# Parking 384 more floats of kept V in PSUM and in the pT tiles while the first MLP streams its weights

## Chip, cores and metric

One NeuronCore of a Trainium2 chip. The metric is the time of one execution in device microseconds (us). A *float* below is one 4-byte number in each of the 128 partitions, so a stretch of n floats is n x 512 bytes.

## What is computed

Two rounds of the same attention block and the same gated MLP on a batch of 4 tokens of width 640. All inputs are float32. The caches and the weights are the same in both rounds.

```python
def attention(x):                       # 32 heads of 128, the last W=1024 rows of the cache
    q = (x @ wq).reshape(B, 1, 32, 128).transpose(0, 2, 1, 3)
    k, v = k_cache[:, :, -W:], v_cache[:, :, -W:]
    p = softmax(einsum("bhqd,bhkd->bhqk", q, k) * 128 ** -0.5)
    o = einsum("bhqk,bhkd->bhqd", p, v)
    return o.transpose(0, 2, 1, 3).reshape(B, 1, 4096) @ wo
def mlp(x):                             # F = 1728
    gate, up = x @ W_gate, x @ W_up
    return (gate * (gate > 0) * up) @ W_down
for _ in range(2):
    x = x + attention(layernorm(x))
    x = x + mlp(layernorm(x))
```

## The kernel before

**What is streamed.** Nearly all the work is reading weights and caches from HBM. The host lays them out in three rows of floats per partition: `heads` (255,744 floats: W_q, K, V and W_o of 27 heads, in the order of their use), `kept` (47,360 floats: the same of the last five heads) and `mlp` (25,920 floats). Layer 0 and layer 1 each read `heads` and `mlp`. `kept` is read once, in layer 0, and stays on the chip until layer 1 has used it. The first `HELD` = 4288 floats of `heads`, a piece of W_q, go to a tile of their own, `first_q`, and stay there for layer 1 too.

**The ring.** Everything else goes through one tile, `store`, of `STORE` = 50,624 floats. Before the kernel is written out, a list `plan` is made of (layer, row, from, to, place in `store`): the pieces, one DMA each, in the order in which they are loaded. `load()` (lines 212 to 221) issues the next piece on SyncE's (SP's) queue as soon as no float of its place in `store` is still in use (`live`). `done()` marks what a matmul has just read as free and calls `load()`. So the order of the DMAs is fixed. On the chip SP takes them one by one, and an issue that waits for TensorE (PE) to finish with a place keeps all later ones waiting.

**The kept part and the first MLP.** In layer 0's MLP `kept` fills 47,360 of the 50,624 floats (`FRONT` is its end). The MLP's 25,920 floats have to pass through what is left, and three stretches of `kept` are moved out of the way for that time: `AHEAD` (768 floats, moved to `probs`), `BACK` (1600 floats of V, moved to the PSUM tile `ps` and to idle columns of `po` and `yy`) and `AWAY` (1408 floats of V just below `BACK`, moved to `parked`, which is 640 columns of the PSUM tile `pp`, and to 384 columns in each of the two `banks`). ScalarE (ACT) makes all these copies. `AWAY` is copied out at the end of layer 0's attention (lines 463 and 529 to 532, then `free(*AWAY)`) and back into `store` late in the MLP (lines 609 to 613); `BACK` comes back in layer 1. The pieces of the MLP are listed by hand in `gu` (used twice for the gate and up weights), `gu_end` and `wd` (W_down); together 7040 floats of places are in rotation. After them come the first pieces of layer 1's `heads`, written out the same way.

**pT.** `pT` is a pair of SBUF tiles of 140 columns that hold the transposed probabilities; VectorE (DVE) writes four columns of each sixteen (line 450), and the columns between must be zero. They are idle from the end of layer 0's attention until layer 1's first values.

**Engines.** PE multiplies; DVE and ACT do softmax, norms and copies; GpSimd (POOL) does nothing after the start.

Of the kernel before, what the change touches and what calls it, by code (L numbers as in the profile page):

```python
# [13 lines left out]
B, D, H, DH, W, F = 4, 640, 32, 128, 1024, 1728  # L14
P = 128
# [44 lines left out]

HELD = 4288
STORE = 50624
FRONT = KEPT * 2 * (D + KV)
# [3 lines left out]
BACK = FRONT - 2 * KV - 1600, FRONT - 2 * KV  # L67
AWAY = BACK[0] - 1408, BACK[0]
HOME = 12992
# [38 lines left out]
def decode_kernel(ctx: ExitStack, tc: tile.TileContext, x, source, sel, out):  # L108
# [60 lines left out]

    f, z, a, q, k = FRONT, STORE - D, AHEAD[0], AWAY[0], BACK[0]  # L170
    assert STORE - FRONT == 2 * 1280 + 64 + D
    gu = [(z, D), (f, 1280), (f + 1280, 1344), (a, 768), (k, 960), (k + 960, 640), (q, 1408)]
    gu_end = [(f, 1280), (f + 1280, 1280), (f + 2560, D)]
    wd = [(a, D), (k, 960), (k + 960, D), (q, 1280), *gu_end, (a, D), (k, D), (k + D, D)]
    lo = 0
# [5 lines left out]

    lo = HELD
    for to, n in (f, 1280), (f + 1280, 1280), (f + 2560, D + 64), (a, 768), (k, 1600):
        put(1, "heads", to, lo, lo + n)
        lo += n
# [112 lines left out]
    pp = ps_p.tile([P, 2, 512], F32, name="pp")  # L298
    parked = pp.rearrange("p j n -> p (j n)")[:, 256:896]
    po = ps_o.tile([P, 512], F32, name="po")  # L300
# [115 lines left out]
    def scores(layer, g):  # L416
        n = len(HEADS[g])
        to = sc[g] = pp if layer and g == order[1][0] else ps
        for i, h in enumerate(HEADS[g]):
            for j in range(2):  # L420
                for b in range(B):
                    lo = (j * B + b) * 512
                    at = SIDE - 1 + SIDE * (B * i + b) - i
                    product(to[32 * b:32 * b + SIDE, j, :], qT[:, at:at + SIDE], *part(layer, "k", h, lo, 512),
                            start=i == 0, stop=i == n - 1, tile_position=(0, 32 * b))
                    part_done(layer, "k", h, lo, 512)
                    if to is pp and k0 + i * KV + lo < HOME + BACK[1] - BACK[0] <= k0 + i * KV + lo + 512:
                        nc.scalar.copy(store[:, HOME:HOME + 1024], ps.rearrange("p j n -> p (j n)"))
                        nc.scalar.copy(store[:, HOME + 1024:HOME + 1280], po[:, 256:])
                        nc.scalar.copy(store[:, HOME + 1280:HOME + 1600], yy[:, QUARTER:3 * QUARTER])  # L430
        nm[g] = small.tile([P, 1], F32, name="nm", bufs=1)
# [10 lines left out]
    def values(layer, g, last=False):  # L442
# [18 lines left out]
        if last and layer == 0:  # L461
            nc.scalar.copy(po[:, 256:], store[:, BACK[0] + 1024:BACK[0] + 1280])
            nc.scalar.copy(parked, away[:, :640])
            free(*BACK)
# [26 lines left out]
    def attention(layer):  # L491
# [12 lines left out]
        for before, g, after, then in zip([None] + gs, gs, gs[1:] + [None], gs[2:] + [None] * 2):  # L504
            totals(g)
            turned()
            if layer == 0 and after is None:
                nc.scalar.copy(probs[:, QUARTER:QUARTER + 768], store[:, AHEAD[0]:AHEAD[1]])
                nc.scalar.copy(ps.rearrange("p j n -> p (j n)"), store[:, BACK[0]:BACK[0] + 1024])
                nc.scalar.copy(yy[:, QUARTER:3 * QUARTER], store[:, BACK[1] - 320:BACK[1]])  # L510
                free(*AHEAD)
# [17 lines left out]
        if layer == 0:  # L529
            for i in range(2):  # L530
                nc.scalar.copy(banks[i][:, P:], away[:, 640 + 384 * i:1024 + 384 * i])
            free(*AWAY)
            project(layer, gs[-2])
# [3 lines left out]
    def forward(layer):  # L537
# [71 lines left out]
        if layer == 0:  # L609
            nc.scalar.copy(away[:, :640], parked)  # L610
            for i in range(2):
                nc.scalar.copy(away[:, 640 + 384 * i:1024 + 384 * i], banks[i][:, P:])
            live[AWAY[0]:AWAY[1]] = [True] * 1408
        down(1)
# [64 lines left out]
```

## Time and profile before

| | |
|---|---|
| time, median of 3 runs | 731.91 us (731.81 to 732.6) |
| the profiled execution's own time | 731.96 us |
| its span (first to last instruction) | 730.2 us |
| read from HBM | 310.57 MB |
| PE busy | 443.9 us (61%) |
| DVE, ACT busy | 76.1 us, 54.5 us |

The profile lists the busy time of each engine, the DMA queues with their bytes and packets, and the chain of work that ended last. The trace beside it answers for any stretch: the busy time of each engine, the mean busy share of the 16 DMA engines and what they moved, who waited for whom, and for a DMA the time from its issue on SP to its landing. The profiled execution took 731.96 us with a span of 730.2 us, so 1.76 us lie outside the span.

### The profile page before, as it was taken

Reading aid. Unit: us, or ns where it says so; the run is one execution under the profiler, and the core shown is the slowest. Engines: PE = TensorE matmul, PEld = TensorE weight load, DVE = VectorE, ACT = ScalarE, POOL = GpSimd, SP = SyncE. Lnnn points to the kernel's source line nnn. Section 1 sums busy time; section 2 is a strip of 40 time slices with the busy share of each in tenths; the row PEclk is TensorE's granted clock in tenths of the full one; section 3 lists DMA queues with packets and bytes.
Section 4 is the critical chain, followed back from the end, with each engine's and each line's share of the span. In section 5 each row is a group of like instructions: output and inputs, shape, how many; then the busy total and the mean of one; then the engine's idle time right before and its main releaser. Section 6 shows DMA issues by size and latency. Waiting matters only on the chain.

```text
span 730.2 us, 8291 instructions
## 1 busy us (share of the span) xinstructions
PE 443.9 (61%) x3776; PEld 147.1 (20%) x3776; DVE 76.1 (10%) x277; ACT 54.5 (7%) x101; POOL 0.2 (0%) x4
## 2 busy tenths in 40 slices
PE   0845665654646565519878896365656556555576
PEld 0211111111111111103344241021111112111233
DVE  1110001010010101002111211001010010101011
ACT  0200000000000000000412210000000000000110
POOL 0000000000000000000000000000000000000000
PEclk9976788877777776759999999677777778878899
DMA  9999999999999999999999999999999999999996
GB/s 409 446 393 446 442 439 437 419 436 439 432 428 429 417 456 424 443 413 429 420 409 396 432 429 446 442 436 424 432 431 443 436 430 423 446 432 432 416 427 286
DMA packets 13290, 311.17 MB, mean 426 GB/s; under 512 B 1476, under 2 KB 1732, under 8 KB 6984
## 3 DMA queue, kind: packets, MB, share of 16 engines
q1 hardware_dynamic: 13104, 310.56, 99.0%
q8 instruction: 29, 0.48, 0.2%
q10 hardware_dynamic: 152, 0.09, 0.1%
q14 instruction: 5, 0.04, 0.0%
HBM read 310.57 MB, written 0.08 MB: 425 GB/s over the span
## 4 chain that ended last, share of the span: by engine, by line
DMA 77%; PE 20%; another core or an unknown queue 1%; issue 1%; DVE 0%; ACT 0%; SPq 0%; DVEq 0%; ACTq 0%
DMA store<-in_heads 60%; PE ps L252 9%; DMA store<-in_kept 8%; DMA store<-in_mlp 8%; PE po L252 5%; PE m L252 2%; PE y L252 1%; PE pp L252 1%; PE pp L440 1%; PE m L411 1%; PE m L477 0%; PE m L468 0%; PE m L349 0%; PE y L379 0%
## 5 line engine op out<-in xcount | busy, mean ns | idle before, releaser
L252 PE MATMUL po<-store,pT 128*16 128x512 f32 (+1 forms) x1026 | 156.0, 716 | 122.4 <-DMA store<-in_heads 117.0
L252 PE MATMUL ps<-store,qT 128*4 128x512 f32 (+3 forms) x996 | 151.0, 687 | 109.5 <-DMA store<-in_heads 87.9
L252 PEld LDWEIGHTS po<-store,pT 128*16 128x16 f32 x1026 | 34.4, 110 | 230.8 <-issue 110.7
L252 PEld LDWEIGHTS ps<-store,qT 128*4 128x4 f32 x996 | 30.0, 93 | 213.2 <-DMA store<-in_heads 98.9
L432 DVE TENSOR_REDUCE nm<-ps 128x1 f32<-128x1024 f32 x17 | 20.8, 1225 | 241.0 <-PE ps L252 241.0
L436 ACT ACTIVATE probs<-ps,nm 128x1024 f32<-128x1024 f32 x17 | 18.9, 1114 | 327.2 <-DVE nm L432 327.2
L252 PE MATMUL m<-store,xT 128*32 128x512 f32 (+4 forms) x150 | 29.0, 580 | 10.5 <-DMA store<-in_heads 10.3
L450 DVE COPY pT<-pp 128x16 f32<-128x16 f32 x128 | 17.2, 169 | 137.5 <-PE po L252 137.5
L460 ACT COPY gates<-po 128x512 f32<-128x512 f32 x18 | 10.5, 586 | 268.3 <-PE po L252 268.3
L252 PE MATMUL y<-store,oT 128*4 128x160 f32 x514 | 22.8, 309 | 9.6 <-DMA store<-in_heads 8.4
L440 PE MATMUL pp<-sel_sb,probs 128*128 128x128 f32 x144 | 20.4, 289 | 0.0
L470 DVE RECIPROCAL r<-m 128x16 f32<-128x16 f32 x18 | 4.6, 258 | 132.2 <-PE m L468 132.2
L440 PEld LDWEIGHTS pp<-sel_sb,probs 128*128 128x128 f32 x144 | 17.9, 151 | 0.0
L252 PE MATMUL pp<-store,xT 128*32 128x256 f32 (+3 forms) x172 | 14.3, 417 | 4.7 <-DMA store<-in_mlp 4.7
L252 PEld LDWEIGHTS y<-store,oT 128*4 128x4 f32 x514 | 12.7, 88 | 17.3 <-DMA store<-in_heads 8.8
L404 DVE TENSOR_SCALAR gates<-m,rstd 128x512 f32<-128x512 f32 (+2 forms) x18 | 12.4, 690 | 24.3 <-PE m L252 24.0
L477 PE MATMUL m<-sel_sb,gates 128*128 128x128 f32 x72 | 11.8, 291 | 1.1 <-ACT gates L460 1.1
L411 PE MATMUL m<-sel_sb,gates 128*128 128x128 f32 x64 | 12.4, 318 | 0.0
L327 PE MATMUL y<-probs,sel_sb 4*4 4x160 f32 x8 | 0.7, 445 | 18.0 <-DMA sel_sb<-in_sel 18.0
L411 PEld LDWEIGHTS m<-sel_sb,gates 128*128 128x128 f32 x64 | 7.7, 157 | 19.2 <-issue 18.8
L252 PE MATMUL y<-store,gates 128*4 128x160 f32 x192 | 9.6, 299 | 2.4 <-DMA store<-in_mlp 2.2
L252 PEld LDWEIGHTS m<-store,xT 128*32 128x32 f32 x150 | 6.2, 116 | 22.0 <-DMA store<-in_heads 12.5
(79 smaller groups left out, 143.5 us busy)
## 6 DMA issues: line engine op xcount, KB each, us to landing
store<-in_heads SPq DMA_DIRECT2D x17, 7936.0 KB, 45.8
store<-in_heads SPq DMA_DIRECT2D x2, 8160.0 KB, 44.5
store<-in_heads SPq DMA_DIRECT2D x2, 8128.0 KB, 35.9
store<-in_heads SPq DMA_DIRECT2D x2, 7968.0 KB, 36.3
store<-in_heads SPq DMA_DIRECT2D x1, 8096.0 KB, 26.3
store<-in_heads SPq DMA_DIRECT2D x1, 7424.0 KB, 44.1
store<-in_heads SPq DMA_DIRECT2D x1, 7360.0 KB, 35.4
store<-in_heads SPq DMA_DIRECT2D x1, 7168.0 KB, 35.1
```

The source lines that it names most:

```text
L252: nc.tensor.matmul(out[:, a:z], by, t[rows, p:p + z - a], start=start and not a, stop=stop and z == n, **how)
L327: nc.tensor.matmul(y[32 * g:32 * g + B], ident[:B, :B], probs[:B, g * QUARTER:(g + 1) * QUARTER], start=True, stop=True, tile_position=(0, ...
L404: nc.vector.tensor_scalar(gates[:, :len(HEADS[g]) * P], qp.pop(g), rstd, SCALE, op0=ALU.mult, op1=ALU.mult)
L411: nc.tensor.transpose(qt[:, i], gates[:, i * P:(i + 1) * P], ident)
L432: nc.vector.tensor_reduce(nm[g], to.rearrange("p j n -> p (j n)"), axis=AX.X, op=ALU.max, negate=True)
L436: nc.scalar.activation(probs, sc.pop(g).rearrange("p j n -> p (j n)"), AF.Exp, bias=nm.pop(g), accum_out=sums[g])
L440: nc.tensor.transpose(pp[:, c // 4, c % 4 * P:c % 4 * P + P], probs[:, c * P:(c + 1) * P], ident)
L450: nc.vector.tensor_copy(to[:, 4 * j:4 * j + 4], pp[:, j].rearrange("p (c x) -> p c x", c=4)[:, :, i:P:32])
L460: nc.scalar.copy(gates, po)
L470: nc.vector.reciprocal(r[g], so.rearrange("p (b i) -> p i b", b=B)[:, :SIDE])
L477: nc.tensor.transpose(ot[:, 127 * b:127 * b + P], gates[:, b * P:(b + 1) * P], ident)
```

## The change

`first_q` grows by 384 floats (`HELD` 4288 to 4672), and `store` shrinks by the same (`STORE` 50,624 to 50,240). To keep 7040 floats of places in rotation during the first MLP, `AWAY` grows by 384 floats (1408 to 1792). They go to 128 more columns of `pp` (`parked` is now 768 columns) and to the first 128 columns of each `pT`; after the copy back those columns are set to zero on POOL, since layer 1 wants them zero. The hand-written pieces follow the new places. Which floats of `BACK` and `AWAY` go to which PSUM tile is also reordered.

```diff
-HELD = 4288
-STORE = 50624
+HELD = 4672
+STORE = 50240
...
-AWAY = BACK[0] - 1408, BACK[0]
+AWAY = BACK[0] - 1792, BACK[0]
...
-    assert STORE - FRONT == 2 * 1280 + 64 + D
-    gu = [(z, D), (f, 1280), (f + 1280, 1344), (a, 768), (k, 960), (k + 960, 640), (q, 1408)]
-    gu_end = [(f, 1280), (f + 1280, 1280), (f + 2560, D)]
-    wd = [(a, D), (k, 960), (k + 960, D), (q, 1280), *gu_end, (a, D), (k, D), (k + D, D)]
+    assert STORE - FRONT == 2 * 1280 + 320
+    gu = [(z, D), (f, 1152), (f + 1152, 1088), (a, 768), (k + 448, 1152), (k - D, 1088), (q, 1152)]
+    gu_end = [(f, 1408), (f + 1408, 1472), (k - 512, 320)]
+    wd = [(a, D), (k, 960), (k + 960, D), (q, 1280), (f, 1280), (f + 1280, 1280), (f + 2560, 320), (k, 320), (a, D),
+          (k + 320, D), (k + 960, D)]
...
-    for to, n in (f, 1280), (f + 1280, 1280), (f + 2560, D + 64), (a, 768), (k, 1600):
+    for to, n in (f, 1280), (f + 1280, 1280), (f + 2560, 320), (a, 768), (k, 1600):
         put(1, "heads", to, lo, lo + n)
...
-    parked = pp.rearrange("p j n -> p (j n)")[:, 256:896]
+    parked = pp.rearrange("p j n -> p (j n)")[:, 256:]
...
-            nc.scalar.copy(parked, away[:, :640])
+            nc.scalar.copy(parked, away[:, 1024:])
             free(*BACK)
...
             for i in range(2):
-                nc.scalar.copy(banks[i][:, P:], away[:, 640 + 384 * i:1024 + 384 * i])
+                nc.scalar.copy(banks[i][:, P:], away[:, 256 + 384 * i:640 + 384 * i])
+            for i in range(2):
+                nc.scalar.copy(pT[i][:, :P], away[:, P * i:P * i + P])
             free(*AWAY)
...
-            nc.scalar.copy(away[:, :640], parked)
+            nc.scalar.copy(away[:, 1024:], parked)
             for i in range(2):
-                nc.scalar.copy(away[:, 640 + 384 * i:1024 + 384 * i], banks[i][:, P:])
-            live[AWAY[0]:AWAY[1]] = [True] * 1408
+                nc.scalar.copy(away[:, 256 + 384 * i:640 + 384 * i], banks[i][:, P:])
+                nc.scalar.copy(away[:, P * i:P * i + P], pT[i][:, :P])
+                nc.gpsimd.memset(pT[i][:, :P], 0.0)
+            live[AWAY[0]:AWAY[1]] = [True] * (AWAY[1] - AWAY[0])
```

On ACT, between the last values of layer 0's attention and the norm ahead of the MLP, these copies stand before (`m` is the pair of banks; line 357 is the norm's first copy):

```order
L462 COPY po<-store 128x256 [waits Activation_49]
L463 COPY pp<-store 128x640 [waits DVE_49,PE_49]
L531 COPY m_109<-store 128x384
L531 COPY m_110<-store 128x384 [waits DVE_49]
L357 COPY probs<-y 128x160 [waits DVE_49]
```

and these now:

```order
L463 COPY po<-store 128x256 [waits Activation_49]
L464 COPY pp<-store 128x768 [waits DVE_49,PE_49]
L532 COPY m_109<-store 128x384
L532 COPY m_110<-store 128x384 [waits DVE_49]
L534 COPY pT_98<-store 128x128
L534 COPY pT_99<-store 128x128
L358 COPY probs<-y 128x160 [waits DVE_49]
```

The copy into `pp` is 128 columns wider, and two copies of 128 columns stand ahead of the release of `AWAY` and of the norm's copy. On the way back ACT gains the same two copies, and POOL two memsets.

On SP, where the second round of the gate and up weights ends and W_down begins, the queue holds before:

```order
L221 DMA store<-in_mlp 128x1280 [waits DMAHW5_49,PE_49]
L221 DMA store<-in_mlp 128x1280 [waits DMAHW6_49,DMAHW4_49,PE_49]
L221 DMA store<-in_mlp 128x640
L221 DMA store<-in_mlp 128x640 [waits DMAHW7_49,PE_49]
L221 DMA store<-in_mlp 128x960 [waits DMAHW0_49,PE_49]
L221 DMA store<-in_mlp 128x640 [waits DMAHW1_49,PE_49]
```

and now:

```order
L222 DMA store<-in_mlp 128x1408 [waits DMAHW6_49,DMAHW5_49,PE_49]
L222 DMA store<-in_mlp 128x1472 [waits DMAHW4_49,PE_49]
L222 DMA store<-in_mlp 128x320 [waits DMAHW1_49,PE_49]
L222 DMA store<-in_mlp 128x640 [waits DMAHW7_49]
L222 DMA store<-in_mlp 128x960 [waits DMAHW0_49,PE_49]
L222 DMA store<-in_mlp 128x640
```

The third piece of this stretch went to the end of `store`, which was free by then; now it is 320 floats that go into `AWAY` (`k - 512`) and wait until PE has read that place, with the pieces for `AHEAD` and `BACK` behind it. In all SP issues 92 DMAs where it issued 91: 28 for the first MLP where there were 27, and otherwise as many as before.

## Rows read from the trace of the kernel before

**Rows 1.** The page: busy time, DMA busy share in 40 slices, DMA totals and queue.

```profile
PE 443.9 (61%) x3776; PEld 147.1 (20%) x3776; DVE 76.1 (10%) x277; ACT 54.5 (7%) x101; POOL 0.2 (0%) x4
DMA  9999999999999999999999999999999999999996
q1 hardware_dynamic: 13104, 310.56, 99.0%
HBM read 310.57 MB, written 0.08 MB: 425 GB/s over the span
```

**Rows 2.** Windows by stage: us, busy us by engine, PEclk, DMA share, GB/s.

```profile
0.00:2.00 2.00, 0.00 (x0) 0.00 (x0) 0.96 (x5) 0.00 (x0) 0.20 (x4) 1.00 0.37 74
2.00:350.00 348.00, 193.77 (x1449) 57.70 (x1450) 33.13 (x117) 19.99 (x33) 0.00 (x0) 0.78 1.00 432
350.00:400.00 50.00, 41.45 (x509) 20.05 (x507) 6.66 (x26) 12.43 (x27) 0.00 (x0) 1.00 1.01 407
400.00:700.00 300.00, 187.15 (x1480) 58.10 (x1483) 31.08 (x115) 19.14 (x33) 0.00 (x0) 0.81 1.00 433
```

**Rows 3.** The page: the chain that ended last, by engine.

```profile
DMA 77%; PE 20%; another core or an unknown queue 1%; issue 1%; DVE 0%; ACT 0%; SPq 0%; DVEq 0%; ACTq 0%
```

**Rows 4.** SP's own queue in 100 to 300 us: packets, MB, share of 16 engines.

```profile
q1 hardware_dynamic: 1673, 86.33, 99.8%
```

**Rows 5.** The same in 350 to 400 us, where the first MLP streams.

```profile
q1 hardware_dynamic: 5132, 20.28, 100.4%
```

**Rows 6.** ACT's timeline around the first MLP: start us, us, what, idle before.

```profile
354.37 0.83 ACT L508 COPY probs<-store 128x768 f32<-128x768 f32 x1 [0.49 <-PE pp L440]
...
362.18 0.69 ACT L463 COPY pp<-store 128x640 f32<-128x640 f32 x1
362.80 0.89 ACT L531 COPY m<-store 128x384 f32<-128x384 f32 x2
365.23 0.29 ACT L357 COPY probs<-y 128x160 f32<-128x160 f32 x1 [1.54 <-DVE ones L356]
...
396.48 0.29 ACT L357 COPY probs<-y 128x160 f32<-128x160 f32 x1 [5.20 <-DVE ones L356]
```

**Rows 7.** The chain in order of time, from the first MLP on: start us, us, what.

```profile
362.26 8.50 DMA store<-in_mlp
...
415.53 0.09 DVE pT L450
```

**Rows 8.** Groups by line and shape: memsets of DVE and POOL, mean ns of one.

```profile
L295 DVE MEMSET pT<- 128x140 f32 x2 | 0.3, 175 | 0.0
...
L669 POOL MEMSET const-float32-0.0<- 128x1 f32 x1 | 0.1, 98 | 0.2 <-issue 0.2
```

**Rows 9.** SP issues near the start of W_down, single windows: start us, us, what.

```profile
377.89 0.42 SPq L221 DMA_DIRECT2D store<-in_mlp  x1
...
379.55 0.33 SPq L221 DMA_DIRECT2D store<-in_mlp  x1
...
380.80 0.33 SPq L221 DMA_DIRECT2D store<-in_mlp  x1
```

**Rows 10.** DMA issues of single windows: KB, us from issue to landing.

```profile
store<-in_mlp SPq DMA_DIRECT2D x1, 320.0 KB, 7.0
...
store<-in_heads SPq DMA_DIRECT2D x1, 640.0 KB, 5.3
...
out_x<-probs SPq DMA_DIRECT2D x1, 80.0 KB, 1.6
```

**Rows 11.** Windows of 1 us in the first MLP and at the end, columns as in rows 2.

```profile
376.00:377.00 1.00, 0.47 (x11) 0.37 (x12) 0.00 (x0) 0.00 (x0) 0.00 (x0) 1.00 0.80 319
...
396.00:397.00 1.00, 0.83 (x16) 0.60 (x13) 0.36 (x2) 0.29 (x1) 0.00 (x0) 1.00 0.91 343
...
723.00:724.00 1.00, 0.35 (x12) 0.32 (x16) 0.00 (x0) 0.00 (x0) 0.00 (x0) 1.00 0.64 261
...
725.00:726.00 1.00, 0.80 (x20) 0.47 (x24) 0.00 (x0) 0.00 (x0) 0.00 (x0) 1.00 0.36 141
```

More of the change, by code (lines that the diff above doesn't have):

```diff
@@ L427, in scores @@
                     if to is pp and k0 + i * KV + lo < HOME + BACK[1] - BACK[0] <= k0 + i * KV + lo + 512:
-                        nc.scalar.copy(store[:, HOME:HOME + 1024], ps.rearrange("p j n -> p (j n)"))
-                        nc.scalar.copy(store[:, HOME + 1024:HOME + 1280], po[:, 256:])
-                        nc.scalar.copy(store[:, HOME + 1280:HOME + 1600], yy[:, QUARTER:3 * QUARTER])
+                        nc.scalar.copy(store[:, HOME + 576:HOME + 1600], ps.rearrange("p j n -> p (j n)"))
+                        nc.scalar.copy(store[:, HOME:HOME + 256], po[:, 256:])
+                        nc.scalar.copy(store[:, HOME + 256:HOME + 576], yy[:, QUARTER:3 * QUARTER])
         nm[g] = small.tile([P, 1], F32, name="nm", bufs=1)
@@ L461, in values @@
         if last and layer == 0:
-            nc.scalar.copy(po[:, 256:], store[:, BACK[0] + 1024:BACK[0] + 1280])
-            nc.scalar.copy(parked, away[:, :640])
+            nc.scalar.copy(po[:, 256:], store[:, BACK[0]:BACK[0] + 256])
+            nc.scalar.copy(parked, away[:, 1024:])
             free(*BACK)
@@ L508, in attention @@
                 nc.scalar.copy(probs[:, QUARTER:QUARTER + 768], store[:, AHEAD[0]:AHEAD[1]])
-                nc.scalar.copy(ps.rearrange("p j n -> p (j n)"), store[:, BACK[0]:BACK[0] + 1024])
-                nc.scalar.copy(yy[:, QUARTER:3 * QUARTER], store[:, BACK[1] - 320:BACK[1]])
+                nc.scalar.copy(ps.rearrange("p j n -> p (j n)"), store[:, BACK[1] - 1024:BACK[1]])
+                nc.scalar.copy(yy[:, QUARTER:3 * QUARTER], store[:, BACK[0] + 256:BACK[0] + 576])
                 free(*AHEAD)
```

## The prediction

> **What bounds the kernel.** I read the page's busy shares first. PE works 61% of the span, DVE 10% and ACT 7%, while SP's DMA queue holds 99.0% of 16 engines' span, and its 40 slices all read 9 but the last [rows 1]. The chain that ended last confirms it: 77% DMA, 20% PE [rows 3]. Then I asked whether the DMA engines are full in every stage or only on average. The windows say: 0.37 in the first 2 us, then 1.00, 1.01 and 1.00 up to 700 us [rows 2]. So it makes no difference for the end that the chain runs over PE for a while at the layer boundary: the queue is full there too. A change moves the end only by the bytes and packets that it takes from the DMA engines, or by leaving them without work. The start (2 us) and the way from the last landing to the end hold nothing that the change touches.
>
> **Bytes removed.** 384 floats more of W_q stay, so 384 x 512 = 196,608 bytes are not read again in layer 1. All else is read as often as before. The stages on both sides of the first MLP move 432 and 433 GB/s and the MLP itself 407 [rows 2]. The bytes go from the stream of layer 1's heads, so I take 432: 0.455 us. At 407 it would be 0.483.
>
> **One DMA more.** SP issues 92 DMAs for 91. The queue's 13,104 packets [rows 1] make 13,104 / 91 = 144 for each DMA: a row for each of 128 partitions and 16 more. The price of a packet comes from two stretches. In 100 to 300 us, with large packets, the queue held 99.8% of 16 x 200 us = 3194 engine-us for 86.33 MB [rows 4], or 27.03 GB/s for one engine. In the MLP it held 100.4% of 16 x 50 us = 803 engine-us for 20.28 MB [rows 5], which at 27.03 GB/s would be 750. The other 53 engine-us over 5132 packets are 10.3 ns each. So a DMA more costs 144 x 10.3 / 16 = 93 ns on each engine. The bound below is 0, if small packets cost nothing here. The bound above is the 1.6 us that the lone output DMA takes from issue to landing [rows 10]. I take 0.093, since that is measured where the new piece stands and with a full queue as there. The other pieces keep their number, so their new sizes cost nothing.
>
> The Trainium skill, page "DMA: Bandwidth & Descriptors", section "Anatomy of one DMA — SWDGE (gpsimd) path", speaks against this price: it fits a DMA's time as about 2.0 us fixed plus its bytes, and the page asks for large transfers. By that, as an estimate, the change would end near 731.96 - 0.46 + 2.0 = 733.5. The trace doesn't agree for a queued DMA: the share of 1.01 in the MLP leaves no room for 2 us after each piece.
>
> **ACT copies, out.** Ahead of the release of AWAY the copy into pp grows from 640 columns (0.69 us) to 768 (0.83 for such a copy), 0.14 more, and two copies of 128 columns are added. One of 160 columns takes 0.29 [rows 6], so 128 take less. The sum is 0.14 to 0.72 us. What is queued behind is the norm's copy at 365.23, ahead of which ACT idles 1.54 us waiting for DVE [rows 6]. So it isn't late. The release of AWAY, and with it SP's next issues, comes up to 0.7 us later. It now holds back two pieces (1088 and 1152 floats), where it held one of 1408. But the piece issued at 362.26 lands 8.50 us later [rows 7], so much is still queued. Even without the 832 floats that now wait (1.05 us at 407 GB/s) the queue has over 5 us left. Cost nothing; without that cover it would be up to the 0.7.
>
> **ACT and POOL, back.** The same additions stand ahead of 5.20 us of ACT idle [rows 6]. POOL sets two tiles of 128 columns to zero. A POOL memset of one column takes 98 ns and DVE's of 140 columns 175 [rows 8]; POOL shows none of this width, so I allow up to 1 us for each. DVE's first write into pT waits for it, and that write is at 415.53 [rows 7], over 20 us later. Cost nothing.
>
> **The held-back piece.** This is the step that can go wrong. The 320-float piece for AWAY waits until PE has read the MLP's stream up to float 12,160, and SP holds the 640 floats for AHEAD behind it, though their place is free. The two pieces after that need float 12,672 anyway. The reads that matter are seen in the trace by what they released: the issue at 379.55 needed float 11,904, that at 380.80 float 12,416 [rows 9]. So this issue falls at about 380.2. What is queued by then ends at float 16,960. The piece issued at 377.89, which ends at 17,280, took 7.0 us [rows 9, 10], so it landed at 384.9, and float 16,960 lands near 384.5. That leaves 4.3 us of queue; the issue for AHEAD follows 0.4 us later [rows 9]. A DMA with nothing ahead of it needs 1.6 us from issue to landing [rows 10], so 2.7 us remain in hand. The 16 engines aren't in step, though: the share falls to 0.80 for one microsecond at 376, and to 0.91 at 396 [rows 11], so the engines that run ahead already find their queues empty now and then. I put this at zero for the sum, since the engines that run behind set the landing, and keep three dips such as that at 376 (3 x 0.2 = 0.6 us) as the bound above.
>
> **The layer boundary.** The first three pieces of layer 1's heads lose the 384 floats (704 become 320), while PE frees their places at the same times as before. The queue there is the shallowest that I found, 5.3 us from issue to landing [rows 10]. It becomes 0.46 to 0.48 us shallower for the pieces behind the shortened one: about 4.8 us against the 1.6. Cost nothing.
>
> **Sum.** 731.96 - 0.455 + 0.093 = 731.60 for the profiled execution. The median of the runs is 0.05 lower, so I forecast 731.55 us, 0.05% under the time before. A measurement of this kernel can't tell that from none: I call faster or slower what differs by over 0.2%, which is 1.46 us.
>
> **Rivals.**
> 1. *The gain is lost among the 16 engines.* The end is the landing on the last engine, not the mean. At 723 us the share is already 0.64, and two microseconds later some engines are still busy, at 0.36 [rows 11]. Other packet sizes shift which engine is last, and new dips come with the held-back piece. For it: the dips exist. Against it: the bytes are taken from all engines alike. Time 731.6 + 0.2 to 0.8 = 731.8 to 732.4. Chance 0.14.
> 2. *The held-back piece empties the queue (slower).* It decides from the point where PE reaches float 12,160 later than 1.6 us before the queue's end, that is 2.7 us later than I work out. Then the engines stand for a DMA's issue to landing, 1.6, and three more issues of 0.4 each [rows 9] follow before the queue has depth again: 2.8 us, so 731.6 + 2.8 = 734.4. Against it: PE reads within the same few microseconds in which data lands. Chance 0.04.
> 3. *Each DMA has a fixed cost that the queue doesn't hide.* 731.96 - 0.455 + 1.6 = 733.1, in 0.2% still. Against it is the full share over 50 us with pieces of a few hundred KB [rows 5]. The page named above would make this the rule. Chance 0.02.
> 4. *Faster.* The reordered pieces remove the dips and let the 16 engines end together. Between 723 and 726 us less than half of the engines' time is used (0.64 falling to 0.36 [rows 11]), so some 1.5 us is in it: 731.6 - 1.5 = 730.1. Nothing in the change aims at the engines one by one. Chance 0.02.
>
> The change can hardly fail to do what it says: with 384 floats fewer in the plan, HBM reads must fall by 0.20 MB, from 310.57 [rows 1] to 310.37.
>
> **How the numbers follow.** The forecast, 731.0 to 732.0, has 0.78. Its low end is the saving at 407 GB/s with a free DMA more (731.4), and 0.4 us if the last engine gets luckier than the mean. With rival 1 the range is 731.0 to 732.4 and holds about 0.92; without rival 1 it would hold less than 8 in 10. Faster by over 0.2%: 0.02 (rival 4). Slower: 0.04 (rival 2). Same: 0.94.
>
> **What would show it.** The page after: HBM read 310.37 MB, 92 x 144 = 13,248 packets in SP's queue, share 1.00 in all stages. The 320-float piece issued near 380 us, and the share from 380 to 385 near 1. ACT's norm copy still waiting for DVE ahead of the MLP. It would be wrong if the share between 380 and 400 us fell to 0.8 for several microseconds, or if the last landings lay further apart than now.

## The result, and the profile after

The changed kernel takes **734.99 us** (median of 7 runs, 734.3 to 736.18) where the kernel before takes 732.14 on the same chip (7 runs, 731.81 to 732.82): a ratio of 1.0038, 95% interval 1.0026 to 1.005. It is 2.85 us slower, and the forecast was 731.55 with a range up to 732.4. The profiled execution took 736.18 us, 4.22 more than that of the kernel before; its span is 734.4.

The page of the changed kernel, the lines that answer to [rows 1] and [rows 3]:

```profile
PE 441.8 (60%) x3776; PEld 148.8 (20%) x3776; DVE 76.1 (10%) x277; ACT 55.5 (8%) x105; POOL 0.6 (0%) x6
...
DMA  9999999999999999998999999999999999999996
...
q1 hardware_dynamic: 13248, 310.37, 98.6%
...
HBM read 310.37 MB, written 0.08 MB: 423 GB/s over the span
...
DMA 76%; PE 21%; another core or an unknown queue 1%; issue 1%; DVE 0%; SPq 0%; ACT 0%; DVEq 0%; ACTq 0%
```

The bytes are as foretold, 310.37 MB, and so are the packets, 13,248. But the DMA row has an 8 that wasn't there, in its nineteenth slice, which begins at 330 us: before the first MLP, in layer 0's last part. The windows by stage of the changed kernel, with the columns of [rows 2]:

```profile
2.00:350.00 348.00, 194.26 (x1449) 59.86 (x1450) 33.15 (x117) 19.99 (x33) 0.00 (x0) 0.79 0.99 429
350.00:400.00 50.00, 38.34 (x464) 17.97 (x459) 4.88 (x21) 11.47 (x26) 0.41 (x2) 1.00 1.01 405
400.00:700.00 300.00, 185.71 (x1505) 59.73 (x1505) 32.53 (x118) 21.10 (x37) 0.00 (x0) 0.82 1.00 431
```

The first 348 us move 429 GB/s for 432 before: 3 x 348 = 1.04 MB less, or 2.4 us at 432 GB/s. So most of the loss has happened ahead of everything that the prediction looked at. Windows of 1 us, of the kernel before and then of the changed one (the last two columns are the DMA share and GB/s):

```profile
332.00:333.00 1.00, 1.00 (x12) 0.19 (x8) 0.00 (x0) 0.00 (x0) 0.00 (x0) 1.00 1.04 449
333.00:334.00 1.00, 1.00 (x14) 0.29 (x10) 0.30 (x1) 0.00 (x0) 0.00 (x0) 1.00 1.02 438
334.00:335.00 1.00, 1.00 (x32) 0.67 (x31) 1.00 (x3) 0.00 (x0) 0.00 (x0) 1.00 0.93 399
335.00:336.00 1.00, 1.00 (x16) 0.25 (x12) 0.35 (x5) 0.98 (x1) 0.00 (x0) 1.00 0.99 426
336.00:337.00 1.00, 1.00 (x16) 0.35 (x12) 0.17 (x1) 0.22 (x2) 0.00 (x0) 1.00 0.99 426
```

```profile
332.00:333.00 1.00, 1.00 (x16) 0.21 (x12) 0.00 (x0) 0.00 (x0) 0.00 (x0) 1.00 0.54 229
333.00:334.00 1.00, 1.00 (x10) 0.20 (x2) 0.11 (x1) 0.00 (x0) 0.00 (x0) 1.00 0.15 66
334.00:335.00 1.00, 1.00 (x30) 0.72 (x32) 1.00 (x1) 0.00 (x0) 0.00 (x0) 1.00 0.08 33
335.00:336.00 1.00, 1.00 (x20) 0.28 (x16) 0.54 (x6) 0.80 (x1) 0.00 (x0) 1.00 1.42 373
336.00:337.00 1.00, 1.00 (x12) 0.23 (x8) 0.17 (x1) 0.41 (x2) 0.00 (x0) 1.00 0.16 53
```

In these five microseconds the kernel before moves 449 + 438 + 399 + 426 + 426 = 2138 KB (1 GB/s for 1 us is 1 KB), the changed one 229 + 66 + 33 + 373 + 53 = 754. The 1384 KB that are missing take 3.2 us at 432 GB/s.

What SP waited for between 290 and 345 us, its longest row in the kernel before and in the changed one (us in all, times, longest), and then the issue of the 6,656-float piece of `kept` in both (start us, us):

```profile
SPq L221 <- PE po L252: 32.2, 4, 26.0
```

```profile
SPq L222 <- PE y L253: 34.5, 1, 34.5
```

```profile
301.46 0.33 SPq L221 DMA_DIRECT2D store<-in_kept  x1
```

```profile
334.62 0.33 SPq L222 DMA_DIRECT2D store<-in_kept  x1
```

DMA issues of the changed kernel from 295 us on, KB and us to landing (in the kernel before the same two took 37.5 and 42.0):

```profile
store<-in_kept SPq DMA_DIRECT2D x1, 4096.0 KB, 36.1
store<-in_kept SPq DMA_DIRECT2D x1, 3328.0 KB, 11.5
```

The piece goes out 33 us later, because it waits for PE's output projection (y, L253) instead of for products with V (po). Only the 4096 KB piece issued at 299.82 was still queued ahead of it, and that landed at 335.9. The chain of the changed kernel in that stretch, in order of time, says why the projection is so late:

```profile
284.00 42.29 DMA store<-in_kept
326.29 0.04 issue
326.33 7.47 PE ps L253 x48
333.81 0.37 PE m L412 x2
334.18 1.20 PE y L253 x32
...
```

PE projects the heads of one group only after the scores of the next group, and those need kept K that lands at 326.29. The piece of `kept` goes to places 26,880 to 33,536. Before, the piece of `heads` that lies there began with float 226,176 at place 20,736, so that place 33,536 is float 238,976: the end of a group's V, just ahead of its W_o. With STORE changed, `turn` moves from 211,840 to 212,352, and the piece at place 20,736 begins with float 226,688. Place 33,536 is then float 239,488, and the piece overwrites the first 512 floats of W_o. SP issues in order, so the rest of `kept` stood behind that wait.

### The profile page after: what moved, and what is told of

Its sections match the earlier page's. It is cut to its first block, busy times and chain, and to the rows that moved or that the text cites. A ratio compares the mean times of both kernels' runs of the same rounds, so it can differ in the third digit from the quotient of the medians.

```text
span 734.4 us, 8297 instructions
## 1 busy us (share of the span) xinstructions
PE 441.8 (60%) x3776; PEld 148.8 (20%) x3776; DVE 76.1 (10%) x277; ACT 55.5 (8%) x105; POOL 0.6 (0%) x6
## 3 DMA queue, kind: packets, MB, share of 16 engines
q1 hardware_dynamic: 13248, 310.37, 98.6%
HBM read 310.37 MB, written 0.08 MB: 423 GB/s over the span
## 4 chain that ended last, share of the span: by engine, by line
DMA 76%; PE 21%; another core or an unknown queue 1%; issue 1%; DVE 0%; SPq 0%; ACT 0%; DVEq 0%; ACTq 0%
DMA store<-in_heads 59%; PE ps L253 9%; DMA store<-in_kept 9%; DMA store<-in_mlp 8%; PE po L253 5%; PE m L253 2%; PE y L253 1%; PE pp L253 1%; PE pp L441 1%; PE m L412 1%; PE m L478 0%; PE m L469 0%; SPq L222 0%; PE m L342 0%
## 5 line engine op out<-in xcount | busy, mean ns | idle before, releaser
L253 PE MATMUL po<-store,pT 128*16 128x512 f32 x1030 | 153.7, 701 | 136.2 <-DMA store<-in_heads 129.1
L253 PE MATMUL ps<-store,qT 128*4 128x512 f32 (+3 forms) x996 | 152.9, 687 | 106.0 <-DMA store<-in_heads 84.8
L253 PEld LDWEIGHTS po<-store,pT 128*16 128x16 f32 x1030 | 34.8, 109 | 241.4 <-issue 112.8
L253 PEld LDWEIGHTS ps<-store,qT 128*4 128x4 f32 x996 | 30.6, 94 | 209.8 <-DMA store<-in_heads 95.7
L253 PE MATMUL m<-store,xT 128*32 128x512 f32 (+4 forms) x146 | 28.2, 583 | 10.6 <-DMA store<-in_heads 10.5
L253 PE MATMUL y<-store,oT 128*4 128x160 f32 x512 | 23.1, 312 | 1.5 <-DVE oT L482 1.1
L253 PEld LDWEIGHTS y<-store,oT 128*4 128x4 f32 x512 | 12.9, 89 | 9.9 <-issue 4.4
L253 PE MATMUL pp<-store,xT 128*32 128x256 f32 (+3 forms) x172 | 11.7, 370 | 5.1 <-DMA store<-in_mlp 5.1
L253 PE MATMUL y<-store,gates 128*4 128x160 f32 x192 | 9.6, 299 | 3.5 <-DMA store<-in_mlp 3.4
L253 PE MATMUL po<-store,xT 128*32 128x256 f32 (+3 forms) x148 | 9.3, 330 | 2.4 <-DMA store<-in_mlp 1.9
```

Source lines behind the costliest of these rows:

```text
L253: nc.tensor.matmul(out[:, a:z], by, t[rows, p:p + z - a], start=start and not a, stop=stop and z == n, **how)
```

## Experiments: the late piece

Theory A: the piece of `kept` that waits for W_o empties the queue and costs the 2.85 us. Theory B, the rival: the first MLP's new pieces, the held-back one above all, and the layer boundary cost it. Four kernels on one chip, beside the kernel before at 732.07 us (21 runs). The first is the changed kernel unaltered.

> The changed kernel again, unaltered, beside the others on one chip. Theory A (one of the pieces of kept, 6656 floats, now waits for W_o to be read and the DMA engines run dry near 333 us): the DMA share falls under 0.2 for two microseconds between 332 and 337 us as in the first profile, idle time there about 2.4 us of all 16 engines, time 2 to 3.5 us over the kernel before. Theory B (the smaller pieces of the first MLP and the uneven DMA engines cost it): the dip at 333 need not come back, the loss lies after 360 us.

Measured: 735.26 us, ratio 1.0040 (1.0028 to 1.0053). It is the 3.2 us that the others are held against. The gap is there again: from 333 to 335 us the DMA share is 0.08 and 0.15.

The second moves one cut in the changed kernel, so that the piece ends where V ends:

```diff
-    put(0, "kept", k0, k0, k1, v0, v0 + 6656, v1, v1 + KV, v1 + 7168, FRONT)
+    put(0, "kept", k0, k0, k1, v0, v0 + 6144, v1, v1 + KV, v1 + 7168, FRONT)
```

> The changed kernel with one cut of kept moved, from v0 + 6656 to v0 + 6144, so that the piece's place ends where the V ahead of W_o ends, as in the kernel before. Theory A: the piece is issued near 301 us, the share stays near 1 from 328 to 340 us, and the time falls by 2.4 us or more against the changed kernel, to within 0.6 us of the kernel before (731.5 to 732.7). Theory B: the time stays 2 to 3 us over the kernel before.

Measured: 733.2 us (11 runs), ratio 1.0016 (1.0007 to 1.0025). Of the loss 2.06 us are gone, and the piece goes out at 301.00 us. That is less than theory A asked for (2.4 us or more, and 731.5 to 732.7 us). Its longest wait in 290 to 345 us, and its windows at the old gap:

```profile
SPq L222 <- PE po L253: 31.6, 3, 25.9
```

```profile
333.00:334.00 1.00, 1.00 (x13) 0.14 (x5) 0.00 (x0) 0.00 (x0) 0.00 (x0) 1.00 0.69 295
334.00:335.00 1.00, 1.00 (x26) 0.69 (x30) 0.98 (x1) 0.00 (x0) 0.00 (x0) 1.00 1.01 434
```

The third puts the fault into the kernel before, whose W_o begins 512 floats later:

```diff
-    put(0, "kept", k0, k0, k1, v0, v0 + 6656, v1, v1 + KV, v1 + 7168, FRONT)
+    put(0, "kept", k0, k0, k1, v0, v0 + 7168, v1, v1 + KV, v1 + 7168, FRONT)
```

> The kernel before with the same cut moved the other way, from v0 + 6656 to v0 + 7168, so that its piece's place reaches into W_o; nothing else is changed. Theory A: the piece is issued near 334 us, the share falls under 0.2 near 333 us, and the time rises by 2 to 3 us (734 to 735). Theory B: no change (within 0.5 us of the kernel before).

Measured: 734.57 us, ratio 1.0034 (1.0022 to 1.0047), 2.5 us slower with nothing else of the change in it. The same wait and the same gap are there:

```profile
SPq L221 <- PE y L252: 34.3, 1, 34.3
```

```profile
332.00:333.00 1.00, 1.00 (x13) 0.11 (x5) 0.00 (x0) 0.00 (x0) 0.00 (x0) 1.00 0.61 262
333.00:334.00 1.00, 1.00 (x26) 0.72 (x26) 0.86 (x1) 0.00 (x0) 0.00 (x0) 1.00 0.08 33
```

Taken away and put in, the cut moves 2.1 and 2.5 us: theory A holds for the bulk. But the mended kernel is 1.1 us over the kernel before, where the prediction wants it 0.36 under. The fourth kernel has the mended cut and no held-back piece:

```diff
-    gu_end = [(f, 1408), (f + 1408, 1472), (k - 512, 320)]
-    wd = [(a, D), (k, 960), (k + 960, D), (q, 1280), (f, 1280), (f + 1280, 1280), (f + 2560, 320), (k, 320), (a, D),
-          (k + 320, D), (k + 960, D)]
+    gu_end = [(f, 1408), (f + 1408, 1472), (a, 320)]
+    wd = [(a + 320, 448), (k + 448, 1152), (k - D, 1088), (q, 832), (f, 1280), (f + 1280, 1280), (f + 2560, 320),
+          (a, 768), (k + 448, 1152), (k, 320)]
```

> As the kernel with the cut at v0 + 6144, and the pieces at the end of the gate and up weights and of W_down laid out anew: the 320-float piece goes to AHEAD's place, which is free early, so that no piece waits long at the head of SP's queue, and 27 DMAs serve the first MLP instead of 28. If the held-back piece costs what the share lost there after the change (0.56 us of all engines from 385 to 405 us, 0.35 in the kernel before): 0.1 to 0.4 us under the kernel with the cut alone. If the engines that run ahead lose nothing that counts: the same within 0.2 us. Against the kernel before, by the sum of the prediction without the DMA more: 0.45 us faster.

Measured: 732.85 us, ratio 1.0011 (1.0002 to 1.002). By the medians the held-back piece, with the W_down pieces that change beside it, is worth 0.35 us, less than these runs resolve, and 0.8 us over the kernel before are left.

## Experiments: where the rest is

Four kernels beside the kernel before at 732.08 us (32 runs). The first makes the ring 384 floats shallower at the layer boundary and does nothing else (theory C):

```diff
-    for to, n in (f, 1280), (f + 1280, 1280), (f + 2560, D + 64), (a, 768), (k, 1600):
+    for to, n in (f, 1280), (f + 1280, 1280), (f + 2560, 320), (a, 768), (k, 1600):
```

> The kernel before with one size changed: layer 1's third piece of `heads` is 320 floats instead of 704, so the ring is 384 floats shallower at the layer boundary, as in the changed kernel. Bytes, number of DMAs, the MLP's pieces, copies and the kept pieces of layer 0 stay. Theory C (with the cut mended, the changed kernel is still 1.1 us over the kernel before, and from the MLP's end to the layer boundary its landings fall 0.9 us further behind the bytes than the kernel before's): the shallower boundary costs it, so this kernel is 0.5 to 1.5 us slower than before, and the loss shows between 350 and 400 us. Rival: the boundary costs nothing, as the prediction had it, and the time is within 0.3 us of before; then the rest lies in the MLP's pieces or in the copies.

Measured: 732.52 us, ratio 1.0006 (0.9997 to 1.0015): 0.44 us, not yet told apart from none, and between what theory C (0.5 to 1.5) and its rival (0.3 at most) expected. The next has the copies and memsets alone:

```diff
-AWAY = BACK[0] - 1408, BACK[0]
+AWAY = BACK[0] - 1792, BACK[0]
...
+                nc.scalar.copy(away[:, P * i:P * i + P], pT[i][:, :P])
+                nc.gpsimd.memset(pT[i][:, :P], 0.0)
```

> The kernel before with the 384 floats parked in the changed kernel's way (pp's wider copy, two copies of 128 floats out of pT and back, two memsets on POOL, the other order of the copies), but W_q's stay and the ring as before: the 384 floats gained are left unused. It prices the copies alone. The prediction has them at nothing: within 0.2 us of before. Rival: they hold up the down projection or the first scores of layer 1, which frees places later, and are the rest of 1.1 us that the mended cut leaves; then this kernel is about 1 us slower than before.

Measured: 732.15 us, ratio 0.9999 (0.9991 to 1.0008). The copies cost nothing. The next uses their space for a deeper ring in the MLP:

```diff
-    gu = [(z, D), (f, 1280), (f + 1280, 1344), (a, 768), (k, 960), (k + 960, 640), (q + 384, 1408)]
+    gu = [(z, D), (f, 1280), (f + 1280, 1344), (a, 768), (k, 960), (k + 960, 640), (q, 1792)]
...
-    wd = [(a, D), (k, 960), (k + 960, D), (q + 384, 1280), *gu_end, (a, D), (k, D), (k + D, D)]
+    wd = [(a, D), (k, 960), (k + 960, D), (q, 512), *gu_end, (a, D), (k, D), (k + D, D)]
```

> The kernel with the copies alone, but with the 384 floats used: in the first MLP's first two laps the ring's last piece is 1,792 floats instead of 1,408, and its last one in the third lap 512 instead of 1,280. Bytes and number of DMAs as before, layer boundary as before; the matmuls of some column groups are split at other places. If a deeper ring in the MLP gives the transfers cover, up to 0.5 us faster than the kernel with the copies alone, and the first version that beats the kernel before; if the MLP's landings follow the bytes already, within 0.3 us of it; if the shallower third lap counts, up to 0.5 us slower.

Measured: 732.49 us, ratio 1.0005 (0.9997 to 1.0014): no gain. The last of the four prices a DMA:

```diff
-            nc.sync.dma_start(out=store[:, to:to + hi - lo], in_=source[row][:, lo:hi])
+            mid = lo + (hi - lo) // 128 * 64 if hi - lo > 4096 else hi
+            for b, e in ((lo, mid), (mid, hi)):
+                if b < e:
+                    nc.sync.dma_start(out=store[:, to + b - lo:to + e - lo], in_=source[row][:, b:e])
```

> The kernel before with every piece of the store over 4,096 floats issued as two DMAs of half the size, one right after the other: some 45 DMAs more, the same bytes, places and waits. It measures the price of a DMA in a full queue. By the prediction's price of packets (9 packets on each engine at 10.3 ns, 0.093 us a DMA) it is 4 us slower or less, since the packets of large pieces may only be cut otherwise; by a fixed cost of a DMA of about 1.6 us, the shortest from issue to landing in the trace, it would be some 70 us slower. If it is the same within 1 us, a DMA more costs next to nothing as long as others are queued behind it.

Measured: 733.8 us, ratio 1.0023 (1.0014 to 1.0032). Its queue on the page:

```profile
q1 hardware_dynamic: 18864, 310.57, 99.2%
```

That is 5760 packets more, or 40 DMAs of 144. They cost 1.72 us, so 0.043 us for a DMA (0.026 to 0.059 by the interval), half of the 0.093 that the prediction took.

The next three ran beside the kernel before at 731.99 us (27 runs). The first is the kernel with the shallower boundary, and 384 floats are left out of layer 1's load:

```diff
-    lo = HELD
+    lo = HELD + 384
...
+        if row == "heads" and layer and lo < HELD + 384:
+            return first_q, lo - HELD, HELD + 384 - lo
```

> The kernel of the shallower boundary (layer 1's third piece 320 floats), with the bytes taken out of it: layer 1 begins at float 4,672 of `heads`, and the 384 floats of W_q before it are not loaded again; their products use the first 384 floats of `first_q` instead, so this part of the computation is wrong. All of layer 0, its MLP's pieces and the later places of layer 1 are as in the kernel before. If bytes are worth what they take at the rate of the stages (0.455 us), it is 0.45 us faster than the kernel with the shallower boundary alone (732.5 us), about 732.1, and then the 0.8 us that the changed kernel with both mendings has over the kernel before come from layer 0's cuts or the MLP's pieces. If the shallower boundary eats them, it stands at 732.5 to 732.9, as that kernel does.

Measured: 731.91 us, ratio 0.9998 (0.9989 to 1.0007). It lies 0.08 us under the kernel before on its chip, where the kernel with all the bytes lay 0.44 over it on another: a difference of 0.52 us. The second is the fourth kernel of above without the saving of bytes:

```diff
-HELD = 4672
+HELD = 4288
```

> The changed kernel with the mended cut and the other MLP pieces (732.85 us), but `first_q` keeps 4,288 floats as before: the bytes of the kernel before, in the changed kernel's shorter ring, the 384 floats gained left unused. If bytes count as the prediction has them, it is 0.45 us slower than that kernel, about 733.3, or 1.2 us over the kernel before: then the shorter ring costs 1.2 us and the bytes give 0.45 of it back. If it is within 0.2 us of 732.85, the bytes give nothing where the ring is shorter.

Measured: 733.2 us, ratio 1.0017 (1.0009 to 1.0026). It lies 1.21 us over the kernel before, where the kernel with fewer bytes lay 0.78 over it: a difference of 0.43 us. The two differences, 0.52 and 0.43, lie on both sides of the 0.455 us of the prediction. So the bytes count about as it said, though each interval reaches some 0.65 us to either side, and the changed kernel's shorter ring costs 1.2 us with these pieces. The third takes 768 floats from layer 1's first pieces instead of 384:

```diff
-    for to, n in (f, 1280), (f + 1280, 1280), (f + 2560, D + 64), (a, 768), (k, 1600):
+    for to, n in (f, 1280), (f + 1280, 896), (f + 2560, 320), (a, 768), (k, 1600):
```

> The kernel before with layer 1's first pieces cut by 768 floats in all (1,280, 896 and 320 instead of 1,280, 1,280 and 704), twice as much as in the kernel of the shallower boundary. Theory C (the depth of the ring at the layer boundary costs time): at least twice that kernel's 0.44 us, so 0.9 to 2 us slower than before. Rival: the 0.44 us were chance, and this one is within 0.5 us of before.

Measured: 733.38 us, ratio 1.0019 (1.001 to 1.0028). So 384 floats cost 0.44 us and 768 cost 1.39: the depth at the layer boundary isn't free. The last four ran beside the kernel before at 732.15 us (33 runs). The first has the MLP pieces of the fourth kernel, in the kernel with the copies alone:

```diff
-    gu = [(z, D), (f, 1280), (f + 1280, 1344), (a, 768), (k, 960), (k + 960, 640), (q + 384, 1408)]
-    gu_end = [(f, 1280), (f + 1280, 1280), (f + 2560, D)]
-    wd = [(a, D), (k, 960), (k + 960, D), (q + 384, 1280), *gu_end, (a, D), (k, D), (k + D, D)]
+    gu = [(z, D), (f, 1152), (f + 1152, 1088), (a, 768), (k + 448, 1152), (k - D, 1088), (q, 1152)]
+    gu_end = [(f, 1408), (f + 1408, 1472), (a, 320)]
+    wd = [(a + 320, 448), (k + 448, 1152), (k - D, 1088), (q, 832), (f, 1280), (f + 1280, 1280), (f + 2560, 320),
+          (a, 768), (k + 448, 1152), (k, 320)]
```

> The kernel with the copies alone (732.15 us, as before), and of the changed kernel only the cut of the first MLP into pieces, in the form without the held-back piece: bytes, layer 0's places and layer 1's first pieces stay as before. The shorter ring costs 1.2 us in all, 0.44 of it through layer 1's first pieces; this run divides the rest. Theory D (the cut into pieces: the last piece of the MLP goes out 640 floats of work later than before, and 5,760 floats are then outstanding instead of 6,400): 0.5 to 0.9 us slower than before. Rival E (layer 0's last laps, whose W_o and V are cut 512 floats further): within 0.3 us of before.

Measured: 732.63 us, ratio 1.001 (1.0001 to 1.0019), 0.48 us slower. With the boundary's 0.44 that is 0.92 of the 1.2 us of the shorter ring, if the parts add up, which no run shows; for layer 0's other cuts 0.3 us are left, less than the runs resolve. The second is the changed kernel with the mended cut, and cuts the MLP so that each lap of the ring takes the places in one order. These lists stand in it for those of the changed kernel:

```diff
+    gu = [(z, D), (f, 1280), (f + 1280, 960), (a, 768), (k, 960), (k + 960, D), (q, 896), (q + 896, 896)]
+    gu_end = [(f, 1280), (f + 1280, 1280), (f + 2560, 320), (a, 768)]
+    wd = [(k, 512), (k + 512, 1088), (q, 832), (q + 832, D), (f, 1280), (f + 1280, 1280), (f + 2560, 320), (a, 768),
+          (k, 512), (k + 512, D), (k + 1152, 320)]
```

> The changed kernel with the mended cut, and the first MLP cut anew so that each lap of the ring takes its places in one order (31 pieces instead of 28): after the last piece 6,400 floats are outstanding, as in the kernel before. By theory D it gains on the kernel with both mendings (732.85 us) what the late last piece costs, 0.3 to 0.8 us less 0.1 for the added DMAs, so 732.1 to 732.6. By rival E it stays at 732.7 to 733.

Measured: 731.94 us, ratio 0.9998 (0.999 to 1.0007). This is the whole change with its fault mended and its pieces cut anew, and it stands 0.21 us under the kernel before, the same within the measurement and under the 732.1 to 732.6 that were expected. With 0.455 us of bytes saved, only some 0.25 us of the shorter ring's 1.2 are left, so most of that price hangs on how the pieces are cut. The third cuts layer 1's first pieces finer in the kernel before:

```diff
-    for to, n in (f, 1280), (f + 1280, 1280), (f + 2560, D + 64), (a, 768), (k, 1600):
+    for to, n in (f, D), (f + D, D), (f + 1280, D), (f + 1920, D), (f + 2560, D + 64), (a, 768), (k, D), (k + D, 960):
```

> The kernel before with layer 1's first pieces cut finer (640, 640, 640, 640, 704, 768, 640, 960 instead of 1,280, 1,280, 704, 768, 1,600): a piece goes out when 640 floats are free, so that just before an issue some 4,480 floats are outstanding instead of 3,840. Three DMAs more, 0.04 us each by the run with the halves. If the depth at the layer boundary costs time (theory C), and the lowest point counts, it is 0.3 to 1 us faster than before; if only the depth after an issue counts, it is the same within 0.3 us.

Measured: 731.64 us (11 runs, 731.53 to 731.93), ratio 0.9993 (0.9984 to 1.0002): 0.51 us under the kernel before, the lowest of all, though the interval still holds no change. All 11 runs lie under the median of the 33 of the kernel before. The fourth has both:

```diff
-    for to, n in (f, 1280), (f + 1280, 1280), (f + 2560, 320), (a, 768), (k, 1600):
+    for to, n in (f, D), (f + D, D), (f + 1280, D), (f + 1920, D), (f + 2560, 320), (a, 320), (a + 320, 448), (k, 832), (k + 832, 768):
```

> The changed kernel with the mended cut, the MLP cut in one order as in the run beside it, and layer 1's first pieces cut finer (640 four times, 320, 320, 448, 832, 768). If the lowest point of the ring at the layer boundary counts, it keeps the 0.455 us of bytes and gets back the shallower ring's loss: 731.0 to 731.8 us, 0.3 to 1 us faster than the kernel before. Otherwise as the run with the MLP in one order, 732.2 to 732.9.

Measured: 731.87 us, ratio 0.9999 (0.999 to 1.0007). It lies between the two expectations, and the gains don't add up. So nothing here is shown to beat the kernel before by more than the measurement can tell.

What the depth does is seen in the windows from 390 to 410 us. In order: the kernel before, 384 floats less, 768 floats less, finer pieces:

```profile
390.00:410.00 20.00, 17.77 (x199) 7.03 (x198) 4.71 (x11) 6.57 (x14) 0.00 (x0) 1.00 1.02 400
```

```profile
390.00:410.00 20.00, 17.82 (x199) 7.03 (x199) 4.69 (x11) 6.72 (x14) 0.00 (x0) 1.00 1.00 386
```

```profile
390.00:410.00 20.00, 17.92 (x199) 7.07 (x200) 4.69 (x11) 6.78 (x14) 0.00 (x0) 1.00 1.01 374
```

```profile
390.00:410.00 20.00, 17.89 (x199) 7.09 (x199) 4.70 (x11) 6.72 (x14) 0.00 (x0) 1.00 1.02 404
```

PE does nearly the same work in all four, and the DMA share reads 1.00 to 1.02. The rate alone tells them apart: 14 GB/s less over 20 us are 280 KB, or 0.65 us at 432 GB/s, and 26 less are 1.2 us. They are to be held against the executions that were profiled, which took 1.40 and 1.55 us more than that of the kernel before (733.36 and 733.51 for 731.96), and not against the medians (0.44 and 1.39): the window holds half of the one and most of the other. In this window the kernel in one order moves 389 GB/s, and the last one, which has the finer pieces besides, 385. In that kernel the finer pieces gave nothing back here.

More than the share tells is in the landings. For each DMA the trace records 16 of them, one for each DMA engine. In the kernel before, those of the first MLP's last piece lie between 393.22 and 395.55 us. Those of layer 1's first piece, issued at 392.11, lie between 395.41 and 397.08. From the one piece to the next it is 2.19 us for the landing that comes first and 1.53 for the one that comes last. So the engine that leads stood still for about 0.7 us (an estimate from these two), while the one that trails had work. The depth from issue to landing is that of the engine that trails. Take the distance between first and last landing at the first MLP's last piece, and its smallest value among the next ten pieces. It falls from 2.33 to 1.08 us in the kernel before, from 2.57 to 0.77 with 384 floats less, from 2.67 to 1.09 with 768 less, and from 2.51 to 1.56 with finer pieces. This is one execution each, and 384 and 768 floats don't come in the order of their times.

The distance also counts at the end. The last piece of all lands with its first engine at 722.83 us in the kernel before, at 723.52 with 384 floats less and at 723.66 in the kernel with both. Its last engine is seen in the chain, in the same order (start us, us):

```profile
695.92 30.69 DMA store<-in_mlp
```

```profile
697.29 30.73 DMA store<-in_mlp
```

```profile
695.90 30.48 DMA store<-in_mlp
```

These end at 726.61, 728.02 and 726.38. With 384 floats less, half of the 1.40 us stands in the first landing, and half in how much further the last engine lags. Why the lag is 3.8, 4.5 and 2.7 us stays open.

For the cut of the MLP no window is as clear. From 375 to 390 us, the kernel with the copies alone and the one with those pieces besides:

```profile
375.00:390.00 15.00, 11.51 (x143) 5.24 (x135) 1.33 (x4) 0.74 (x2) 0.00 (x0) 1.00 1.02 410
```

```profile
375.00:390.00 15.00, 10.68 (x131) 4.88 (x124) 1.32 (x4) 1.02 (x3) 0.00 (x0) 1.00 1.01 392
```

Here the loss shows (18 x 15 = 270 KB, 0.6 us), but the same pieces in the changed kernel's ring show it after 395 us (320 GB/s up to 400 us, for 372 in the kernel with the copies alone). Which of the pieces costs the 0.5 us stays open. So does whether theory D has the reason right (the last piece going out 640 floats later): the kernel in one order changes the other pieces too.

## Why the prediction was wrong

**What bounds the kernel** held in that DMA sets the time, and the end moves by bytes and by leaving the engines without work. What didn't hold is that a share of 1.00 means a full queue: the landings show engines that stand still at shares of 1.00 to 1.02. **Bytes removed** held: 310.37 MB, and the two pairs of runs that differ in little but the bytes give 0.43 and 0.52 us for the 0.455 worked out.

**One DMA more** was right in its count, and its price was twice too high: 0.043 us in a full queue, for 0.093, though it is the price for halves of large pieces. The Trainium skill's page "DMA: Bandwidth & Descriptors", section "Anatomy of one DMA — SWDGE (gpsimd) path", with its fixed 2.0 us, would make the 40 DMAs of the halved pieces 80 us, as an estimate, if it were carried over to them. That section is about DMAs issued on GpSimd, while these are issued on SP and queued. They took 1.72, so for a queued DMA of this kernel it doesn't hold. The prediction set the share of 1.01 against it, which proves little, since the share is as high at 374 GB/s. In the same part stands the sentence that failed: *the other pieces keep their number, so their new sizes cost nothing.* A piece's size also sets which reads must be over before it can go out. I followed the new issues in the first MLP and at the layer boundary, where the diff has them. I didn't follow the pieces of layer 0, whose lines the diff doesn't touch, though HELD and STORE move nearly all places of `heads`. The one cut that is written as a number, `v0 + 6656`, had stood exactly at the end of V. The rows of the trace before that would have told it are SP's waits in 290 to 345 us: the piece waited there for po, the products with V, and 512 floats on is another releaser. No rival had this; the time of rival 2, 734.4, comes near by another mechanism.

**The copies and memsets** cost nothing, as forecast. In the changed kernel's timelines the two memsets of POOL, and then ACT's first copy of the norm after the release of AWAY, read (start us, us, idle before):

```profile
395.76 0.20 POOL L617 MEMSET pT<- 128x128 f32 x1 [395.32 <-ACT store L616]
396.34 0.20 POOL L617 MEMSET pT<- 128x128 f32 x1 [0.37 <-ACT store L616]
```

```profile
368.04 0.29 ACT L358 COPY probs<-y 128x160 f32<-128x160 f32 x1 [1.41 <-DVE ones L357]
```

A memset takes 0.20 us, where I allowed up to 1, and ACT still waits for DVE, 1.41 us for 1.54 before [rows 6].

**The held-back piece** did what was foretold, to a smaller depth. It went out at 384.02 us, 3.8 after the foretold 380.2. Not all of that is the time lost earlier: in the kernel with the mended cut it goes out at 381.48, 1.3 us late. It landed 3.7 us later, where 4.3 were foreseen:

```profile
384.02 0.33 SPq L222 DMA_DIRECT2D store<-in_mlp  x1
```

```profile
store<-in_mlp SPq DMA_DIRECT2D x1, 160.0 KB, 3.7
```

The engines do run low behind it. Windows of 2 us of the kernel with the mended cut, which has this piece:

```profile
382.00:384.00 2.00, 1.14 (x13) 0.47 (x12) 0.00 (x0) 0.00 (x0) 0.00 (x0) 1.00 0.92 311
384.00:386.00 2.00, 1.30 (x17) 0.54 (x16) 0.00 (x0) 0.00 (x0) 0.00 (x0) 1.00 1.04 356
```

And the same windows of the kernel with the mended cut and no held-back piece:

```profile
382.00:384.00 2.00, 1.04 (x13) 0.47 (x12) 0.00 (x0) 0.00 (x0) 0.00 (x0) 1.00 1.04 416
384.00:386.00 2.00, 1.39 (x19) 0.94 (x18) 0.00 (x0) 0.17 (x1) 0.00 (x0) 1.00 1.03 383
```

That makes (105 + 27) x 2 = 264 KB, 0.6 us, the upper bound that I gave and didn't take; by the medians it is 0.35. The difference doesn't stay. From 390 to 410 us the kernel with the piece is the faster one, by 21 x 20 = 420 KB:

```profile
390.00:410.00 20.00, 17.78 (x202) 6.68 (x195) 4.44 (x10) 7.24 (x16) 0.41 (x2) 1.00 1.02 399
```

```profile
390.00:410.00 20.00, 18.10 (x209) 7.06 (x207) 4.44 (x10) 6.93 (x16) 0.41 (x2) 1.00 1.00 378
```

So in these two executions, of 732.85 and 733.23 us, the piece decides where the loss falls, and doesn't add to it. The step that failed here is the zero in the sum: I counted on the engines that run behind. From the piece issued at 377.32 us to the one issued at 387.94 the distance between first and last landing falls from 2.44 to 1.24 us in the kernel with the piece, so the engine that leads stood still.

**The layer boundary** was costed at nothing. 768 floats cost 1.39 us there, and 384 cost 0.44 by the medians, which isn't told apart from none. An empty queue, the mechanism that I checked, doesn't occur for the engine that lands last. Of the kernel with the shallower boundary alone, the shortened piece still takes 5 us to land (KB, us from issue to landing):

```profile
store<-in_heads SPq DMA_DIRECT2D x1, 160.0 KB, 5.1
```

The term that I set to zero is what a shallower queue loses while only some engines' queues are empty. That is near **rival 1**, the gain lost among the 16 engines, and the landings show such engines. But its size was too small, and that the gain was lost in this way is argued, not tested: with the fault mended the changed kernel lies at 732.85 to 733.2 us, above its 731.8 to 732.4. Of the sum, then, 2.1 to 2.5 us is the late piece of `kept`, 0.44 the boundary, about 0.5 the cut of the MLP, up to 0.35 the held-back piece, and -0.43 to -0.52 the bytes. These make 2.5 to 3.4 us, where 2.85 and 3.2 were measured. Only the first is shown both ways; the others were measured in different kernels and, as the two windows above show, needn't add up.

## What to carry to other kernels

Where places come out of a plan, a change of one size moves every later place: list, for each transfer before and after, the last read that it waits for, and look at those that change, not at the lines that the diff touches. A cut that ends exactly at the edge of another tensor is such a place. A ring that is made shorter to save bytes can pay them back in depth: here 384 floats of depth at the one shallow place cost 0.44 us by the medians, which isn't resolved, and 384 floats of bytes save 0.455. How the pieces are cut decided more than the depth: with the same shorter ring the kernel stood at 732.85 us with one cut (the kernel before: 732.07) and at 731.94 with another (732.15).

## What the runs showed of the hardware

A DMA share of 1.00 to 1.02 doesn't show that the DMA engines move all they can: in 390 to 410 us it covered 374 to 404 GB/s for the same work and nearly the same PE time. A queue that is still 5 us deep by its last landing loses time when it gets shallower (1.39 us for 768 floats), although a lone DMA needs 1.6 us from issue to landing [rows 10]. The 16 engines run out of step: the 16 landings of one piece lie up to 3.4 us apart ahead of the dry queue of the changed kernel and 1.7 behind it (332.52 to 335.94 us, then 344.36 to 346.09), which fits engines that lead and had to wait. The time scatters more with the shallower ring as well: eleven runs lie within 0.4 us with finer pieces (731.53 to 731.93) and within 2.1 us with 768 floats less (732.48 to 734.59). That engines out of step are the reason for the scatter was not tested. Another DMA in a full queue costs 0.043 us, measured on large pieces cut in two.
